# Linear attention with a routed expert layer: three numerator accumulators, the selection moved to ScalarE, GpSimd's first order bound, and gathered rows transposed as fp32r

## The chip, the cores and the metric

The kernel runs on one core of one Trainium2 chip. A core has TensorE (PE: matrix products; PEld is its load of the stationary operand), VectorE (DVE), ScalarE (ACT), GpSimd (POOL) and SyncE (SP, which issues most transfers). The metric is the time of one execution on the device in microseconds (us); lower is better. A second number, the span, is the time that the trace of a profiled execution covers.

## The reference

Linear attention over 8 batches, 8 heads, 576 positions and head size 64, and behind it a layer of 8 experts in which each of the 4608 rows goes to the one expert with the largest logit.

```python
def phi(x):
    proj = einsum('bhsd,df->bhsf', x, w_phi)                    # 128 features
    proj = proj - max(abs(proj), axis=-1, keepdims=True)
    return concatenate([exp(proj), exp(-proj)], axis=-1)
kv  = einsum('bhsf,bhsd->bhfd', phi(k), v)
z   = sum(phi(k), axis=2)
num = einsum('bhsf,bhfd->bhsd', phi(q), kv)
den = einsum('bhsf,bhf->bhs', phi(q), z)[..., None] + 1e-06
x   = rows of num / den                                          # 4608 x 512
logits = x @ w_gate                                              # 8 experts
expert = argmax(logits); gate = softmax(logits)[expert]
out[row] = gate[row] * (relu(x[row] @ w1[expert]) @ w2[expert])  # 512 -> 1024 -> 512
```

## The kernel before

The attention is cut into 16 units: 4 groups `g` of two batches, and in each group 4 pairs of heads `pr`. Most products run as three products in the type fp32r: a value is split into a rounded part (`xh`, `vh`, `kh`, `wh`) and a residual (`xl`, `vl`, `kl`, `wl`), and high x high, high x low and low x high are summed in PSUM. The rounding is a copy on ScalarE, the residual a subtraction on VectorE or GpSimd.

In a unit, `split` (L243, L244) cuts loaded pieces of q and k into `xh` and `xl`; `project` (L255 to L257) makes the feature projections `ps_proj`; VectorE takes the maximum `mx` (L261) and subtracts it (`t`, L262); ScalarE makes the exponentials `e` (L274, L275), and `k_parts` makes `kh` (L282, ScalarE) and `kl` (L284, on GpSimd for pieces 4 and 6, and for piece 0 from unit 1 on). For q, `t` is transposed on TensorE (`pt`, L293) and ScalarE writes the exponentials `qp`, or `qz` for the last, half chunk. `v_parts` makes `vh` (ScalarE, L311) and `vl` (GpSimd, L312). The products of k and v (`pk`, L336) gather kv for one batch; ScalarE copies them (`kvT`, L353), and a product with `fold` (`pf`, L362: identity columns and a block of `w_gate`) gives `kf`, which VectorE copies. The numerators, 9 chunks of 128 rows by 2 heads, are `pn` (L386; L395 for the tail chunk of both batches). Each has 73 columns: 64 of the result, one denominator, 8 logits. They stand in PSUM accumulators of six slots of 73 columns; one unit fills four (chunks 0 to 2, 3 to 5, 6 and 7, and the tail), and two accumulators exist at a time. `normalize` and `normalize_tail` divide them on VectorE (`rec`, `xrow`, `lgc`; L423 to L458), and `xrow` goes to a table in DRAM.

The routing of a group (`route`) sums the logits of the 4 pairs, takes the expert, counts rows per expert, gives each row its rank, and writes selection matrices: for each of the 9 chunks, `sel_p` on VectorE and `sel_h` on GpSimd (L788), each one comparison of an index row with the chunk's rank `rkr`, times a value. Of the last group's chunks some are written on ScalarE instead (L780 to L782). For the first three groups the routing's steps are `deferred`: they are laid between the products of the units that follow the group (about 150, 250 and 350 us). Only the last group's routing, near 420 to 445 us, stands between two stages.

Then come 17 pair units of two gathered blocks each (256 rows), and single blocks. `x_parts` transposes a gathered block `xg` in four pieces on TensorE into `px` (L1078) and splits it on ScalarE and VectorE (L1080, L1081); the first layer is `pm` (L1098 to L1100), the second `po` (L1118 to L1120), and the weights are split as they arrive (`wh` L1053, `wl` L1054).

A scheduler of the framework sets the order of each engine's instructions from the order of the code, priorities and dependences; `ordered` chains the products of TensorE, and `behind(m, other)` sets an instruction behind another on one engine without a wait. `merge` and `zipped` lay the features of a unit between the products of the one before. `constants` and the first unit's features begin the kernel.

```python
if u % NPR == 0 and u > 0:
    run(deferred)
    deferred = route(st["g"] - 1, units[u - 1]["lgc"], 0, NC)
```

Of the kernel before, what the change touches and what calls it, by code (L numbers as in the profile page):

```python
# [37 lines left out]
NSLOT = 7  # L38
NEARLY = (NG - 1) * NC
# [10 lines left out]
def tile_linear_attention_moe(  # L50
# [20 lines left out]
    make_identity(nc, ident)  # L71
    gidx = keep.tile([P, NB], I32, name="gidx")
# [58 lines left out]
    def constants():  # L131

        G.memset(fold, 0.0)
        for h in range(H):
            G.tensor_copy(fold[:, h, 0 : D + 1], ident[0 : D + 1, 0 : D + 1])
        nc.scalar.dma_start(fold[0:D, :, D + 1 : W], w_gate.rearrange("(h d) e -> d h e", d=D))

    def constants2():

        G.memset(ltri, 1.0)  # L140
        G.affine_select(ltri, ltri, [[1, P]], ALU.is_gt, 0.0, base=0, channel_multiplier=-1)

        G.iota(iota_i, [[1, P]], base=0, channel_multiplier=0)
        G.tensor_copy(iota_p, iota_i)
        G.tensor_copy(iota_pb, iota_i)
        G.tensor_scalar_add(iota_em, iota_e, -float(E))
        G.iota(part_i, [[0, 1]], base=1, channel_multiplier=1)
        G.tensor_copy(part1, part_i)


        G.iota(hb_i[:, :, 0:4], [[18, NG], [2, 4]], base=0, channel_multiplier=0)
        G.iota(hb_i[:, :, 4:8], [[18, NG], [2, 4]], base=9, channel_multiplier=0)
        G.iota(hb_i[0:64, :, 8:9], [[18, NG], [0, 1]], base=8, channel_multiplier=0)
        G.iota(hb_i[64:P, :, 8:9], [[18, NG], [0, 1]], base=16, channel_multiplier=0)
        G.tensor_copy(hbase, hb_i.rearrange("p g c -> p (g c)"))
        G.tensor_scalar_mul(hbase, hbase, 64.0)
        G.tensor_scalar_mul(neg1, part1, -1.0)
        G.tensor_scalar_mul(neg_h, hbase, -1.0)

# [77 lines left out]
    def split(st, x, part, eh, el):  # L237
# [6 lines left out]
        el.tensor_tensor(xl[:, 0:n], xr[:, 0:n], xh[:, 0:n], op=ALU.subtract)  # L244
# [33 lines left out]
    def k_parts(st, c0, n):  # L278
# [5 lines left out]
        eng.tensor_tensor(kl, e[:, 0:m], kh, op=ALU.subtract)  # L284
# [22 lines left out]
    def v_parts(st, u):  # L307
# [4 lines left out]
        G.tensor_tensor(vl, vt, vh[:, :, 0:D], op=ALU.subtract)  # L312
# [65 lines left out]
    def num_steps(st, chunks):  # L378


        def step(c, hh, s):
            if c in (0, 3, 6, 8) and hh == 0 and s == 0:
                st["pn"] = ps_nm.tile([P, 6, W], F32, name="pn")
            qp, s0 = st["qp", c]
            if c < 8:
                m = T.matmul(  # L386
                    st["pn"][:, 2 * (c % 3) + hh, :],
# [5 lines left out]
            else:  # L393

                m = T.matmul(  # L395
                    st["pn"][:, 2 * hh : 2 * hh + 2, :],
# [5 lines left out]
            if c in (2, 5, 7, 8) and hh == 1 and s == 1:  # L402
                if c < 8:
                    normalize(st, c - c % 3, c % 3 + 1, st["pr"])
                else:
                    normalize_tail(st, st["pr"])
# [11 lines left out]
    def normalize(st, c0, n, pr):  # L418
        pn = st["pn"][:, 0 : 2 * n]
        if c0 == 0:  # L420
            st["x"] = hold.tile([P, NC, P], F32, name="xrow", bufs=2)
        rec = sm.tile([P, 6], F32, name="rec", bufs=2)[:, 0 : 2 * n]
        V.tensor_scalar_add(rec, pn[:, :, D], 1e-6)  # L423
        V.reciprocal(rec, rec)
        rb = rec.rearrange("p (c h) -> p c h", h=2).unsqueeze(3)
        V.tensor_tensor(
            st["x"][:, c0 : c0 + n, :].rearrange("p c (h d) -> p c h d", h=2),
            pn[:, :, 0:D].rearrange("p (c h) d -> p c h d", h=2),
            rb.to_broadcast([P, n, 2, D]),
            op=ALU.mult,  # L430
        )
        V.tensor_tensor(
            st["lgc"][:, c0 : c0 + n, 2 * pr : 2 * pr + 2, :],
            pn[:, :, D + 1 : W].rearrange("p (c h) e -> p c h e", h=2),
            rb.to_broadcast([P, n, 2, E]),
            op=ALU.mult,
        )

    def normalize_tail(st, pr):

        pn = st["pn"][:, 0:4].rearrange("p (h b) w -> p h b w", b=2)
        rec = sm.tile([P, 6], F32, name="rec", bufs=2)[:, 0:4].rearrange("p (h b) -> p h b", b=2)
        V.tensor_scalar_add(rec, pn[:, :, :, D], 1e-6)
        V.reciprocal(rec, rec)
        for b in range(2):
            rows = slice(D * b, D * b + D)
            V.tensor_tensor(
                st["x"][rows, 8, :].rearrange("p (h d) -> p h d", h=2),
                pn[rows, :, b, 0:D],
                rec[rows, :, b].unsqueeze(2).to_broadcast([D, 2, D]),  # L450
                op=ALU.mult,
            )
            V.tensor_tensor(
                st["lgc"][rows, 8, 2 * pr : 2 * pr + 2, :],
                pn[rows, :, b, D + 1 : W],
                rec[rows, :, b].unsqueeze(2).to_broadcast([D, 2, E]),
                op=ALU.mult,
            )  # L458
# [188 lines left out]
    def route(g, lgc, c0, n, final=None):  # L647
# [13 lines left out]
        def logits():  # L661
            V.tensor_reduce(
                tile_of("lg", [P, NC, E]),
                lgc[:, c0 : c0 + n].rearrange("p c h e -> p c e h"),
                axis=AX.X,
# [118 lines left out]
        def select(c):  # L784
            if final is not None and c0 + c in ON_ACT:
                return select_a(c)
            for eng, dst, by in ((V, sel_p, part1), (G, sel_h, hbase[:, j0 + c : j0 + c + 1])):
# [129 lines left out]
    for g in range(NG):  # L917
        lgc = sm.tile([P, NC, H, E], F32, name="lgc")
# [150 lines left out]
    def x_parts(u, i):  # L1069
# [7 lines left out]
        for k in range(KD):  # L1077
            T.transpose(px[:, k, :], xg[:, k * P : (k + 1) * P], ident)  # L1078
# [277 lines left out]
```

## Time and profile before

| | |
|---|---|
| time before, median of 3 runs | 924.06 us (922.11 to 924.46) |
| the profiled execution's own time | 923.96 us |
| its span, instructions | 922.3 us, 18298 |
| mean granted clock of TensorE | 0.983 of full speed |
| TensorE busy | 889.5 us, 96% |
| VectorE, ScalarE, GpSimd busy | 596.7, 590.5, 485.0 us |
| attention units, about | 0 to 410 us |
| last numerators and last routing, about | 410 to 455 us |
| pair units, single blocks, about | 455 to 815 us, 815 to 905 us |

The busy time of an engine is the sum of its instructions' durations, overlaps counted once. The granted clock tells at which share of its full speed TensorE was let run: in a stretch with a low number, each product takes longer. In a row of a timeline, the first two numbers are start and duration in us; a bracket behind a row tells how long the engine was idle before it and what ended the idle time. In rows of groups, `x41` is the number of instructions, then come total us and mean ns.

### The profile page before, as it was taken

What the parts mean: (1) busy time and instruction counts of PE and PEld (TensorE: products, weight loads), DVE (VectorE), ACT (ScalarE), POOL (GpSimd) and SP (SyncE); (2) the same over time, 40 slices, a digit from 0 to 9 for tenths busy, and PEclk for the clock granted to TensorE, in tenths of its full rate; (3) what the DMA queues carried; (4) which work ended last, traced back from release to release, by engine and by line L of the source; (5) the groups of instructions that cost most, each with busy time, mean ns of one, the idle gap of its engine ahead of it and who ended that gap; (6) DMA issues with size and microseconds to landing.
All of it is one profiled execution on the core that took longest, in us unless ns stands there. A gap on an engine that the chain in (4) does not pass through costs nothing. (4 is left out here: it accounts for less than half of the span.)

```text
span 922.3 us, 18298 instructions
## 1 busy us (share of the span) xinstructions
PE 889.5 (96%) x6703; PEld 831.0 (90%) x6703; DVE 596.7 (65%) x1134; ACT 590.5 (64%) x900; POOL 485.0 (53%) x332
## 2 busy tenths in 40 slices
PE   7799999999999999999999999999999999999995
PEld 6799999999999999999799999999999999987883
DVE  7477788777987788759774444444444444457850
ACT  7577787777868776755565555555555555568951
POOL 7556668866676669734443333333333333337641
PEclk9799999999999999999999999999999999999998
DMA  5233433233334333243143143431434634764100
GB/s 154 80 96 107 107 106 103 68 100 102 93 93 108 106 107 93 76 129 108 59 154 122 45 152 115 155 112 44 153 114 158 215 113 149 229 206 129 46 24 15
DMA packets 64620, 102.44 MB, mean 111 GB/s; under 512 B 10702, under 2 KB 28622, under 8 KB 64528
## 3 DMA queue, kind: packets, MB, share of 16 engines
q1 hardware_dynamic: 57136, 80.31, 28.5%
q0 software_dynamic: 6720, 20.80, 7.3%
q8 instruction: 53, 0.87, 0.4%
q14 instruction: 39, 0.32, 0.1%
q10 hardware_dynamic: 672, 0.15, 0.1%
HBM read 136.81 MB, written 20.26 MB: 170 GB/s over the span
## 5 line engine op out<-in xcount | busy, mean ns | idle before, releaser
L1054 DVE TENSOR_TENSOR wl<-raw,wh 128x1024 fp32r<-128x1024 f32 x138 | 184.6, 1350 | 136.2 <-ACT wh L1053 136.1
L1053 ACT CAST wh<-raw 128x1024 fp32r<-128x1024 f32 x184 | 191.4, 1050 | 93.7 <-PE po L1120 66.2
L1054 POOL TENSOR_TENSOR wl<-raw,wh 128x1024 fp32r<-128x1024 f32 x46 | 113.3, 2469 | 175.0 <-ACT wh L1053 167.6
L386 PE MATMUL pn<-kf,qp 128*128 128x73 f32 x1024 | 156.8, 252 | 0.0
L1099 PE MATMUL pm<-xl,wh 128*128 128x256 f32 x544 | 154.1, 283 | 0.0
L1100 PE MATMUL pm<-xh,wl 128*128 128x256 f32 x544 | 154.1, 283 | 0.0
L1098 PE MATMUL pm<-xh,wh 128*128 128x256 f32 x544 | 153.4, 283 | 0.0
L386 PEld LDWEIGHTS pn<-kf,qp 128*128 128x128 f32 x1024 | 151.3, 190 | 0.1
L284 POOL TENSOR_TENSOR kl<-e,kh 128x1024 fp32r<-128x1024 f32 x47 | 112.4, 2392 | 50.7 <-ACT kh L282 47.9
L261 DVE TENSOR_REDUCE mx<-ps_proj 128x4 f32<-128x512 f32 (+1 forms) x160 | 101.2, 633 | 43.8 <-PE ps_proj L257 43.1
L244 POOL TENSOR_TENSOR xl<-xr,xh 128x512 fp32r<-128x512 f32 (+2 forms) x63 | 88.0, 1403 | 69.6 <-ACT xh L243 69.5
L1118 PE MATMUL po<-wh,hh 128*128 128x512 f32 x272 | 108.9, 401 | 0.0
L1119 PE MATMUL po<-wl,hh 128*128 128x512 f32 x272 | 106.8, 392 | 1.1 <-DVE wl L1054 1.1
L1099 PEld LDWEIGHTS pm<-xl,wh 128*128 128x128 f32 x544 | 104.1, 191 | 2.8 <-DVE xl L1081 0.4
L1098 PEld LDWEIGHTS pm<-xh,wh 128*128 128x128 f32 x544 | 104.0, 191 | 2.5
L1120 PE MATMUL po<-wh,hl 128*128 128x512 f32 x272 | 106.1, 390 | 0.0
L336 PE MATMUL pk<-kl,vh 128*65 128x256 f32 x320 | 99.8, 312 | 4.9 <-POOL kl L284 4.1
L1100 PEld LDWEIGHTS pm<-xh,wl 128*128 128x128 f32 x544 | 104.1, 191 | 0.2 <-issue 0.2
L262 DVE TENSOR_TENSOR t<-ps_proj,mx 128x512 f32<-128x512 f32 (+1 forms) x160 | 99.9, 632 | 3.2
L336 PE MATMUL pk<-kh,vh 128*65 128x256 f32 x320 | 100.6, 314 | 0.0
L336 PE MATMUL pk<-kh,vl 128*64 128x256 f32 x320 | 100.4, 314 | 0.0
L255 PE MATMUL ps_proj<-w_hi,xh 128*128 128x256 f32 x288 | 90.2, 313 | 4.2 <-DVE t L262 2.4
(232 smaller groups left out, 2010.9 us busy)
## 6 DMA issues: line engine op xcount, KB each, us to landing
raw<-w SPq DMA_DIRECT2D x184, 512.0 KB
vt<-vv SPq DMA_DIRECT2D x15, 640.0 KB
x_dram<-xrow SPq DMA_DIRECT2D x30, 256.0 KB
xr<-kT SPq DMA_DIRECT2D x15, 320.0 KB
xr<-qT SPq DMA_DIRECT2D x15, 320.0 KB
xr<-kT SPq DMA_DIRECT2D x17, 256.0 KB
xr<-qT SPq DMA_DIRECT2D x17, 256.0 KB
x_dram<-xrow SPq DMA_DIRECT2D x32, 32.0 KB
```

Of the source, the lines that this page charges most:

```text
L261: V.tensor_reduce(mx[:, 0 : 2 * n], psv, axis=AX.X, op=ALU.max, apply_absolute_value=True)
L284: eng.tensor_tensor(kl, e[:, 0:m], kh, op=ALU.subtract)
L336: return T.matmul(st["pk", bb][0:n, hh, :], (vl if j == 1 else vh)[:, 2 * (c + (bb if c == 8 else 0)) + hh, 0:n], (kl if j == 2 else kh)[: ...
L386: m = T.matmul(st["pn"][:, 2 * (c % 3) + hh, :], qp[:, s, s0 + hh, :], st["kf"][:, c // 4, hh, s, :], start=(s == 0), stop=(s == 1),)
L1053: A.copy(th, raw[k])
L1054: m = (G if k in (POOL_LO if u else POOL_LO0) else V).tensor_tensor(tl, raw[k], th, op=ALU.subtract)
L1098: T.matmul(pm[:, i], th, xh[:, k, :], start=(k == 0), stop=False)
L1099: T.matmul(pm[:, i], th, xl[:, k, :], start=False, stop=False)
L1100: T.matmul(pm[:, i], tl, xh[:, k, :], start=False, stop=(k == KD - 1))
L1118: T.matmul(po, hh[:, i, r], th[:, c], start=(i == j == 0), stop=False)
L1119: T.matmul(po, hh[:, i, r], tl[:, c], start=False, stop=False)
L1120: T.matmul(po, hl[:, i, r], th[:, c], start=False, stop=(i == 1 and j == 3))
```

## The change

It has four parts.

Three accumulators: a unit's numerators fill three accumulators of seven slots in turn instead of four of six. The index `i = 2 * c + hh` counts chunk and head; the third accumulator holds the last two ordinary slots and the tail's four. `normalize` takes an accumulator's first index and does what `normalize_tail` did too, and `lgc` is laid out by pair, so that the logits' sum runs over two axes.

Selection: in the routing of the first three groups, `sel_p` is written on ScalarE by two activations, `y` = |index - rank| and relu(part - part * y), which is `part` where the index is the rank, and zero elsewhere. `sel_h` stays on GpSimd. The last group's routing keeps its code.

GpSimd's first order: the clearing of `fold` is set behind the residual of k's third part of unit 0, the residual of unit 1's first part of k behind the `kl` of piece 4 of unit 0, and the `vl` of unit 1 behind the `kl` of piece 0.

Transposes: those of the gathered rows read and write their data as fp32r, with an fp32r copy of the identity that is made on GpSimd among the constants.

```diff
+SLOTS = 7
...
+    ident_r = keep.tile([P, P], F32R, name="ident_r")
...
-        G.memset(fold, 0.0)
+        behind(G.memset(fold, 0.0), units[0]["xl", "k", 2])
...
+        G.tensor_copy(ident_r, ident)
...
-        el.tensor_tensor(xl[:, 0:n], xr[:, 0:n], xh[:, 0:n], op=ALU.subtract)
+        m = el.tensor_tensor(xl[:, 0:n], xr[:, 0:n], xh[:, 0:n], op=ALU.subtract)
+        st["xl", x, part] = m
+        if (st["u"], x, part) == (1, "k", 0):
+            behind(m, units[0]["kl", 4])
...
-        eng.tensor_tensor(kl, e[:, 0:m], kh, op=ALU.subtract)
+        st["kl", c0] = eng.tensor_tensor(kl, e[:, 0:m], kh, op=ALU.subtract)
...
-        G.tensor_tensor(vl, vt, vh[:, :, 0:D], op=ALU.subtract)
+        m = G.tensor_tensor(vl, vt, vh[:, :, 0:D], op=ALU.subtract)
+        if u == 1:
+            behind(m, st["kl", 0])
...
-            if c in (0, 3, 6, 8) and hh == 0 and s == 0:
-                st["pn"] = ps_nm.tile([P, 6, W], F32, name="pn")
+            i = 2 * c + hh
+            if i % SLOTS == 0 and c < 8 and s == 0:
+                st["pn"] = ps_nm.tile([P, SLOTS, W], F32, name="pn")
...
-                    st["pn"][:, 2 * (c % 3) + hh, :],
+                    st["pn"][:, i % SLOTS, :],
...
-                    st["pn"][:, 2 * hh : 2 * hh + 2, :],
+                    st["pn"][:, 2 + 2 * hh : 4 + 2 * hh, :],
...
-            if c in (2, 5, 7, 8) and hh == 1 and s == 1:
-                if c < 8:
-                    normalize(st, c - c % 3, c % 3 + 1, st["pr"])
-                else:
-                    normalize_tail(st, st["pr"])
+            if s == 1 and (i % SLOTS == SLOTS - 1 or i == 17):
+                normalize(st, i - i % SLOTS, st["pr"])
+                if c == 8:
...
+    def normalize(st, i0, pr):
...
+        last = i0 == 2 * SLOTS
+        m = 6 if last else SLOTS
+        n = 2 if last else SLOTS
+        rec = sm.tile([P, SLOTS], F32, name="rec", bufs=2)
+        V.tensor_scalar_add(rec[:, 0:m], pn[:, 0:m, D], 1e-6)
+        V.reciprocal(rec[:, 0:m], rec[:, 0:m])
...
+        def divide(rows, dst, slots):
+            k = dst.stop - dst.start
+            r = rec[rows, slots].unsqueeze(2)
+            for t, c0, c1 in ((x, 0, D), (lg, D + 1, W)):
+                V.tensor_tensor(
+                    t[rows, dst], pn[rows, slots, c0:c1], r.to_broadcast([rows.stop - rows.start, k, c1 - c0]), op=ALU.mult
+                )
+
+        divide(slice(0, P), slice(i0, i0 + n), slice(0, n))
+        if last:
+            for b in range(2):
+                divide(slice(D * b, D * b + D), slice(16, 18), slice(2 + b, 6, 2))
...
-            for eng, dst, by in ((V, sel_p, part1), (G, sel_h, hbase[:, j0 + c : j0 + c + 1])):
+            by = hbase[:, j0 + c : j0 + c + 1]
+            if final is None:
+                y = sg.tile([P, P], F32, name="y", bufs=2)
+                A.activation(y, iota_p, AF.Abs, bias=r["rkr"][:, c : c + 1], scale=-1.0)
+                A.activation(sel_p[:, j0 + c, :], y, AF.Relu, bias=part1, scale=neg1)
+            for eng, dst, by in ((G, sel_h, by),) if final is None else ((V, sel_p, part1), (G, sel_h, by)):
...
-        lgc = sm.tile([P, NC, H, E], F32, name="lgc")
+        lgc = sm.tile([P, NPR, 2 * NC, E], F32, name="lgc")
...
-            T.transpose(px[:, k, :], xg[:, k * P : (k + 1) * P], ident)
+            T.transpose(px[:, k, :].bitcast(F32R), xg[:, k * P : (k + 1) * P].bitcast(F32R), ident_r)
```

The order of the instructions moves with it. GpSimd (POOL) at the start, behind the constants; `vl_171` is unit 1's, the `xl` of 640 columns behind it is unit 1's too, and the two `kl` behind are unit 0's. Before:

```order
L156 TENSOR_SCALAR hbase<-hbase 128x36 [waits Pool_49]
L158 TENSOR_SCALAR neg_h<-hbase 128x36 [waits Pool_49]
L244 TENSOR_TENSOR xl<-xr,xh 128x512 [waits DMAHW2_49,PE_49,Activation_49]
L312 TENSOR_TENSOR vl_171<-vt,vh_169 128x1280 [waits DMAHW4_49,Activation_49]
L244 TENSOR_TENSOR xl<-xr,xh 128x640 [waits DMAHW3_49,PE_49,Activation_49]
L284 TENSOR_TENSOR kl<-e,kh 128x1024 [waits Activation_49] x2
L244 TENSOR_TENSOR xl<-xr,xh 128x640 [waits DMAHW5_49,PE_49,Activation_49]
L244 TENSOR_TENSOR xl<-xr,xh 128x512 [waits DVE_49,DMAHW6_49,PE_49,Activation_49]
```

The same place now, where `ident_r` has joined the constants some rows ahead and `vl_172` is unit 1's:

```order
L158 TENSOR_SCALAR hbase<-hbase 128x36 [waits Pool_49]
L160 TENSOR_SCALAR neg_h<-hbase 128x36 [waits Pool_49]
L247 TENSOR_TENSOR xl<-xr,xh 128x512 [waits DMAHW1_49,PE_49,Activation_49]
L290 TENSOR_TENSOR kl<-e,kh 128x1024 [waits Activation_49]
L247 TENSOR_TENSOR xl<-xr,xh 128x640 [waits DMAHW2_49,PE_49,Activation_49]
L247 TENSOR_TENSOR xl<-xr,xh 128x640 [waits DMAHW5_49,PE_49,Activation_49]
L290 TENSOR_TENSOR kl<-e,kh 128x1024 [waits Activation_49]
L247 TENSOR_TENSOR xl<-xr,xh 128x512 [waits DVE_49,DMAHW6_49,PE_49,Activation_49]
L290 TENSOR_TENSOR kl<-e,kh 128x1024 [waits Activation_49]
L247 TENSOR_TENSOR xl<-xr,xh 128x512 [waits PE_49,DMAHW7_49,Activation_49,Pool_49]
L318 TENSOR_TENSOR vl_172<-vt,vh_170 128x1280 [waits DMAHW4_49,Activation_49]
```

The first `kl` of unit 0 has moved ahead of unit 1's `vl` and `xl`, and `vl` stands behind three `kl`.

GpSimd at the first group change, the routing's steps among the residuals of the units around; `onehot`, `base`, `sel_h` and `gt` are the routing's. Before:

```order
L709 CAST onehot<-oh_b 128x72 [waits DVE_49]
L738 TENSOR_TENSOR base<-base,gsum 128x8 [waits DVE_49]
L284 TENSOR_TENSOR kl<-e,kh 128x1024 [waits Activation_49]
L244 TENSOR_TENSOR xl<-xr,xh 128x640 [waits PE_49,DMAHW1_49,Activation_49,Pool_49]
L312 TENSOR_TENSOR vl_168<-vt,vh_166 128x1280 [waits DMAHW4_49,Activation_49]
L244 TENSOR_TENSOR xl<-xr,xh 128x512 [waits PE_49,DMAHW7_49,Activation_49,Pool_49]
L788 TENSOR_SCALAR sel_h<-iota_pb,rkr,hbase 128x128 [waits DVE_49]
L788 TENSOR_SCALAR sel_h<-iota_pb,rkr,hbase 128x128 x4
L284 TENSOR_TENSOR kl<-e,kh 128x1024 [waits Activation_49]
L788 TENSOR_SCALAR sel_h<-iota_pb,rkr,hbase 128x128 x4
L809 COPY gt<-se 128x36 [waits DVE_49]
L244 TENSOR_TENSOR xl<-xr,xh 128x512 [waits PE_49,DMAHW0_49,Activation_49,Pool_49]
```

The same place now:

```order
L701 CAST onehot<-oh_b 128x72 [waits DVE_49]
L730 TENSOR_TENSOR base<-base,gsum 128x8 [waits DVE_49]
L247 TENSOR_TENSOR xl<-xr,xh 128x640 [waits PE_49,DMAHW0_49,Activation_49,Pool_49]
L247 TENSOR_TENSOR xl<-xr,xh 128x640 [waits PE_49,DMAHW1_49,Activation_49,Pool_49]
L290 TENSOR_TENSOR kl<-e,kh 128x1024 [waits Activation_49]
L318 TENSOR_TENSOR vl_169<-vt,vh_167 128x1280 [waits DMAHW2_49,Activation_49]
L785 TENSOR_SCALAR sel_h<-iota_pb,rkr,hbase 128x128 [waits DVE_49]
L785 TENSOR_SCALAR sel_h<-iota_pb,rkr,hbase 128x128 x8
L290 TENSOR_TENSOR kl<-e,kh 128x1024 [waits Activation_49]
L806 COPY gt<-se 128x36 [waits DVE_49]
L290 TENSOR_TENSOR kl<-e,kh 128x1024 [waits Activation_49,Pool_49]
L247 TENSOR_TENSOR xl<-xr,xh 128x512 [waits PE_49,DMAHW7_49,Activation_49,Pool_49]
```

All nine `sel_h` stand ahead of the next `kl`, where five did, and an `xl` of 512 columns has moved behind them.

VectorE (DVE) at the same group change, from the ranks (`blk`, `rkr`) on, with the normalization (`rec`, `xrow`, `lgc`) of the numerators `pn`. Before:

```order
L763 CAST blk<-prki 128x9 [waits DVE_49]
L764 CAST rkr<-prki 128x9
L423 TENSOR_SCALAR rec<-pn 128x6 [waits PE_49]
L788 TENSOR_SCALAR sel_p<-iota_pb,rkr,part_145 128x128 [waits DVE_49]
L788 TENSOR_SCALAR sel_p<-iota_pb,rkr,part_145 128x128
L424 RECIPROCAL rec<-rec 128x6 [waits DVE_49]
L788 TENSOR_SCALAR sel_p<-iota_pb,rkr,part_145 128x128
L426 TENSOR_TENSOR xrow<-pn,rec 128x384 [waits DVE_49]
L432 TENSOR_TENSOR lgc<-pn,rec 128x3x16
L788 TENSOR_SCALAR sel_p<-iota_pb,rkr,part_145 128x128 x3
L423 TENSOR_SCALAR rec<-pn 128x4 [waits PE_49]
```

The same place now:

```order
L755 CAST blk<-prki 128x9 [waits DVE_49]
L756 CAST rkr<-prki 128x9
L268 TENSOR_TENSOR t<-ps_proj,mx 128x512 [waits DVE_49]
L434 TENSOR_SCALAR rec<-pn 128x7 [waits PE_49]
L435 RECIPROCAL rec<-rec 128x7 [waits DVE_49]
L443 TENSOR_TENSOR xrow<-pn,rec 128x448 [waits DVE_49]
L443 TENSOR_TENSOR lgc<-pn,rec 128x56
L267 TENSOR_REDUCE mx<-ps_proj 128x2 [waits PE_49]
L268 TENSOR_TENSOR t<-ps_proj,mx 128x256 [waits DVE_49,Activation_49]
L434 TENSOR_SCALAR rec<-pn 128x6 [waits PE_49]
L435 RECIPROCAL rec<-rec 128x6 [waits DVE_49]
L267 TENSOR_REDUCE mx<-ps_proj 128x2 [waits PE_49]
```

The selections are gone from VectorE, and the normalization of seven slots follows the ranks with one projection's `t` between.

On ScalarE the nine pairs of `y` and `sel_p` stand in ones and twos among the `e`, `qp`, `kh` and `kvT` of that unit, ahead of some of each.

More of the change, by code (lines that the diff above doesn't have):

```diff
@@ L416, in num_steps @@
         ]
-    def normalize(st, c0, n, pr):
-        pn = st["pn"][:, 0 : 2 * n]
-        if c0 == 0:
+    def normalize(st, i0, pr):
+        pn = st["pn"]
+        if i0 == 0:
             st["x"] = hold.tile([P, NC, P], F32, name="xrow", bufs=2)
[L422 to L458, printed above, removed]
+        last = i0 == 2 * SLOTS
@@ new lines, in normalize @@
+        m = 6 if last else SLOTS
[3 more added lines that the diff above has]
+        V.reciprocal(rec[:, 0:m], rec[:, 0:m])
+        x = st["x"].rearrange("p c (h d) -> p (c h) d", h=2)
+        lg = st["lgc"][:, pr]
+        def divide(rows, dst, slots):
[5 more added lines that the diff above has]
+                )
@@ L663, in logits @@
                 tile_of("lg", [P, NC, E]),
-                lgc[:, c0 : c0 + n].rearrange("p c h e -> p c e h"),
-                axis=AX.X,
+                lgc[:, :, 2 * c0 : 2 * c0 + 2 * n].rearrange("p r (c h) e -> p c e r h", h=2),
+                axis=AX.XY,
                 op=ALU.add,
```

## The prediction

> **What bounds the kernel now.** The busy times and the slices of the page come first.
>
> ```profile
> PE 889.5 (96%) x6703; PEld 831.0 (90%) x6703; DVE 596.7 (65%) x1134; ACT 590.5 (64%) x900; POOL 485.0 (53%) x332
> ...
> PE   7799999999999999999999999999999999999995
> ...
> PEclk9799999999999999999999999999999999999998
> ```
>
> TensorE is busy for 889.5 of 922.3 us, so only three things can make the kernel faster: idle time of TensorE, time at a lowered clock, or cheaper work on TensorE. A second list, of what TensorE waited for, names the idle time.
>
> ```profile
> PE pn L395 <- DVE lgc L432: 5.8, 3, 1.9
> PE pk L336 <- POOL kl L284: 4.1, 1, 4.1
> ...
> PE ps_proj L255 <- ACT xh L243: 1.8, 1, 1.8
> ```
>
> The columns are total us, times, longest. Three waits of 1.9 us for a normalization on VectorE, and one of 4.1 us for a residual on GpSimd, lead it. A table of windows shows what they cost (window and length; then busy us of PE, weight loads, DVE, ACT, POOL with instruction counts; then the granted clock, DMA share, GB/s).
>
> ```profile
> 22.00:27.00 5.00, 0.92 (x8) 0.67 (x7) 1.81 (x3) 1.44 (x3) 4.55 (x3) 1.00 0.61 198
> 27.00:31.00 4.00, 4.00 (x23) 3.81 (x21) 1.66 (x3) 2.95 (x5) 1.66 (x1) 0.57 0.02 8
> 31.00:35.00 4.00, 1.55 (x9) 1.14 (x8) 0.57 (x2) 3.92 (x9) 2.27 (x2) 0.87 0.00 0
> 35.00:40.00 5.00, 5.00 (x27) 5.00 (x27) 3.11 (x6) 1.13 (x5) 1.27 (x1) 0.50 0.44 131
> 96.00:120.00 24.00, 23.84 (x223) 23.48 (x223) 18.36 (x43) 18.68 (x33) 15.41 (x9) 1.00 0.39 103
> 152.00:160.00 8.00, 6.06 (x42) 5.86 (x41) 7.00 (x20) 2.80 (x8) 8.00 (x8) 0.80 0.77 226
> 350.00:358.00 8.00, 6.09 (x44) 5.90 (x43) 7.09 (x20) 2.21 (x5) 8.00 (x8) 0.80 0.70 209
> 140.00:165.00 25.00, 23.06 (x206) 22.77 (x205) 21.92 (x61) 16.25 (x31) 21.51 (x18) 0.93 0.34 98
> 600.00:620.00 20.00, 20.00 (x136) 18.50 (x135) 8.27 (x9) 10.33 (x14) 6.87 (x4) 1.00 0.32 107
> ```
>
> A normal attention unit (96 to 120 us) and the pair stage (600 to 620) leave TensorE full at full clock: there only cheaper TensorE work counts. After each wait the clock is cut for a few us: 0.57 and 0.50 in the start, 0.80 over the 8 us of a group change. So a wait costs more than its length. At the group change TensorE issued 42 instructions in 8 us where a normal unit issues 223/24 x 8 = 74, so 32 / 9.3 per us = 3.5 us are lost, three times: 10.5 us.
>
> **Part 1, the selection on ScalarE.** The timeline of VectorE, GpSimd and TensorE at the first group change:
>
> ```profile
> 151.53 3.52 DVE L788 TENSOR_SCALAR sel_p<-iota_pb,rkr,part 128x128 bf16<-128x128 bf16 x2
> 154.97 0.18 DVE L424 RECIPROCAL rec<-rec 128x6 f32<-128x6 f32 x1
> 155.86 0.19 DVE L432 TENSOR_TENSOR lgc<-pn,rec 128x48 f32<-128x48 f32 x1
> ...
> 151.08 2.69 POOL L312 TENSOR_TENSOR vl<-vt,vh 128x1280 fp32r<-128x1280 f32 x1
> 153.74 1.25 POOL L244 TENSOR_TENSOR xl<-xr,xh 128x512 fp32r<-128x512 f32 x1
> 158.99 2.38 POOL L284 TENSOR_TENSOR kl<-e,kh 128x1024 fp32r<-128x1024 f32 x1
> ...
> 156.20 0.49 PE L395 MATMUL pn<-kf,qz 128*128 128x146 f32 x2 [1.94 <-DVE lgc L432]
> 164.50 0.32 PE L336 MATMUL pk<-kl,vh 128*65 128x256 f32 x1
> ```
>
> Two `sel_p` take 3.52 us, and end (155.05) when GpSimd's `vl` and `xl` end (154.99). Behind them wait the reciprocal and `lgc`, and TensorE's tail product, which needs the accumulator back. The same selections, by source line over the group change, and ScalarE's two instructions for one selection, from the final route:
>
> ```profile
> L788 DVE TENSOR_SCALAR sel_p<-iota_pb,rkr,part x9: 300/370/2299, 151.5 to 158.1; 128x128 bf16<-128x128 bf16 x9
> L788 POOL TENSOR_SCALAR sel_h<-iota_pb,rkr,hbase x9: 781/791/1293, 155.0 to 164.2; 128x128 bf16<-128x128 bf16 x9
> ...
> L781 ACT ACTIVATE sel_p<-y,part,neg 128x128 bf16<-128x128 f32 x5 | 2.4, 483 | 0.0
> L780 ACT ACTIVATE y<-iota_p,rkr 128x128 f32<-128x128 f32 x5 | 1.8, 392 | 0.1
> ```
>
> One selection lasts 300 ns beside an idle GpSimd and up to 2299 beside a busy one (minimum, median, maximum). The Trainium skill, "SBUF — State Buffer", section "Who interferes with whom", says that VectorE and GpSimd share a port pair, that a VectorE scalar operation in its two-port mode and a GpSimd instruction exclude each other for a whole instruction, and that ScalarE never waits; the trace agrees in 2299 against 300 ns, and by that rule the selections on ScalarE would wait for nobody.
>
> The change takes all 27 off VectorE, so the place that stalls is gone: up to 10.5 us. What it puts in place: 9 x (0.39 + 0.48) = 7.9 us of ScalarE per group at most. ScalarE has 25.00 - 16.25 = 8.7 us idle in the window of the group change, 3.5 of them in the stall that goes, so 5.2: it fits only by running 2.7 us into the next unit, which has 24.00 - 18.68 = 5.3. Queued behind selections are `kvT`, `e` and `kh`; each pair that is in front costs such a step up to 1 us or so, and TensorE waits for `kvT`.
>
> GpSimd is the closer one: 21.51 busy of 25.00, and with the stall gone 21.5 in 21.5. The nine `sel_h` stand now all ahead of the `kl` that ran at 158.99, before only five. That is 4 x 0.79 = 3.2 us, less the `xl` of 1.25 now behind it: 1.9 us later. It ended at 161.37 and was used at 164.50, 3.1 us of slack, all of it (3.5) lent by the stall. So TensorE may wait up to 1.9 + 0.4 = 2.3 us, or not at all if the queue starts earlier. I take 1.7 given back per group, `kvT` and a little clock included. Gain 3 x (3.5 - 1.7) = 5.4 us; ends: 10.5, and a loss of 3 x 0.8 = 2.4 where a 2.3 us wait costs what 1.94 did and more (4.3 by the same ratio of 3.5/1.94).
>
> **Part 2, three accumulators.** VectorE loses two small instructions per unit, 32 in all, on an engine with 18.36 of 24 busy: nothing on the path. The tail product joins accumulator three, which was given back when the first seven slots had been normalized, long before; so it no longer waits for the normalization just ahead. That secures part 1's gain but adds none in units that had no wait. The last group's route begins after a larger accumulator: up to two products' worth later, plus 0.5 us (ends 0 and 1).
>
> **Part 3, GpSimd's first order.** Timeline of the start:
>
> ```profile
> 18.79 1.30 POOL L244 TENSOR_TENSOR xl<-xr,xh 128x512 fp32r<-128x512 f32 x1
> 20.05 2.72 POOL L312 TENSOR_TENSOR vl<-vt,vh 128x1280 fp32r<-128x1280 f32 x1
> 22.72 1.54 POOL L244 TENSOR_TENSOR xl<-xr,xh 128x640 fp32r<-128x640 f32 x1
> 24.21 2.34 POOL L284 TENSOR_TENSOR kl<-e,kh 128x1024 fp32r<-128x1024 f32 x1
> ...
> 20.39 1.04 ACT L282 CAST kh<-e 128x1024 fp32r<-128x1024 f32 x1
> ...
> 26.61 0.34 PE L336 MATMUL pk<-kl,vh 128*65 128x256 f32 x1 [4.08 <-POOL kl L284]
> 35.44 0.54 PE L362 MATMUL pf<-fold,kvT 65*128 65x73 f32 x2
> ```
>
> `vl` and `xl` of the next unit stand ahead of a `kl` whose `kh` was there at 21.43. Now `kl` comes right behind the first `xl`. With the copy of the identity on the same queue (an estimate of 0.3 us, a quarter of this `xl` of four times its columns, and 1.3 at most) `xl` ends near 20.9, `kl` runs from 21.5 to 23.9, and TensorE goes on at 24.0: 2.6 us earlier. Behind it lies the cut clock: 4 x 0.43 = 1.7 us in 27 to 31 and 5 x 0.50 = 2.5 in 35 to 40, and 4 - 1.55 = 2.45 us idle in 31 to 35. What is late next is `xl` of unit 1 and its `xh` (the 1.8 us wait in the list), which the change doesn't hasten. I count 2.6, a half of the clock loss (2.1) and 0.8 of the second idle stretch: 5.5 us. Ends: 2 (the copy and the memset shift the queue by as much as 0.6 more and every clock loss stays) and 2.6 + 1.7 + 2.5 + 1.2 = 8. The moved memset and `vl` are covered by GpSimd's idle time after 26.5; `fold` is first read at 35.44, in the last row. ScalarE's cast of unit 1's `vh` moves back with `vl` and hastens nothing that is waited for.
>
> **Part 4, transposes as fp32r.** Pair stage, and the groups' rows:
>
> ```profile
> 601.92 0.28 PE L1100 MATMUL pm<-xh,wl 128*128 128x256 f32 x1
> 602.04 0.60 PE L1078 MATMUL px<-ident,xg 128*128 128x128 f32 x4
> 602.40 0.47 PE L1118 MATMUL po<-wh,hh 128*128 128x512 f32 x1
> 602.71 0.40 PE L1119 MATMUL po<-wl,hh 128*128 128x512 f32 x1
> 602.95 0.40 PE L1120 MATMUL po<-wh,hl 128*128 128x512 f32 x1
> ...
> L1078 PE MATMUL px<-ident,xg 128*128 128x128 f32 x164 | 25.0, 273 | 0.8 <-DMA xg<-x_dram,gidx 0.8
> ```
>
> `L1118` leads to the next after 0.31 us instead of 0.24, so four transposes take 0.36 + 0.07 = 0.43 us, 108 ns each, 17.7 us over 164. An fp32r product of 256 columns takes 0.12 us and one of 512 0.24, so 128 columns would take 55 to 60 ns at that rate: at most 164 x 51 ns = 8.4 us saved. The other end is zero: one instruction each before and after, and the weight loads stay. I take the middle, 26 ns each, 4.2 us, since neither an fp32r product of 128 columns nor an fp32 one of 256 stands in the trace to decide it. All of it lies on the path (20.00 busy of 20).
>
> The Trainium skill, "TensorE: Matmul & The Clock Gate", section "LDWEIGHTS (loading the stationary operand)", gives a load as its columns over 1.2 in ns, whatever the type's speed in the array. By it a transpose of 128 columns is bound near 107 ns by its load, part 4 brings nothing, and the sum below would be 913.6; the trace has 108 ns for a transpose, but also 0.12 us for the fp32r product of twice the columns with a load of the same size, so that it cannot decide. The zero is a rival below.
>
> **The sum.** The profiled execution took 923.96 us, 0.1 below the median of 924.06. 923.96 - 5.4 + 0.5 - 5.5 - 4.2 = 909.4.
>
> **Rivals.** First, transposes no cheaper: 913.6. For it: the load of equal size. Against: the load of the fp32r product hides in 0.12 us. Second, transposes at the full fp32r rate: 909.4 - 4.2 = 905.2. Third, the group change brings nothing net: TensorE waits about 1.9 us for `kl` or `kvT` instead of `lgc`, so 909.4 + 5.4 = 914.8. For it: GpSimd full at 21.5 of 21.5. Fourth, on the other side: GpSimd becomes the bound of the route units. Then `kl`, and behind it the two `xl` that the selections push back, are each late, two waits per group with a cut clock each, 2 x 3.5 = 7 us for the 3.5 saved: +10.5, and with part 3 at its low end of 2 and transposes unchanged 933. It decides against the change only where TensorE waits over 1.94 + 5.5/3 x 0.55 = 2.9 us per group, where 0.55 is 1.94/3.5, the wait behind a lost us, and 5.5 is part 3; that is more than the 2.3 us found above. Fifth, nothing acts: the start's wait passes to `xl` and `xh` of unit 1 and the group's to `kl`, transposes unchanged: 923 to 924.
>
> **How the numbers follow.** Chances: forecast 0.42, first rival 0.2, second 0.14, third 0.12, fourth 0.06, fifth 0.06. A measurement here tells a change from none from about 0.3%, 2.8 us. The first four cases lie below 921: 0.88, less 0.02 for their edges; the fifth is no change, with those edges 0.07; the fourth slower, 0.07. The range: low end 899, all four terms near their better ends (8.5, 8 and 8.4 for parts 1, 3 and 4); high end 921, a third rival with a zero in part 4 and 3 us left of part 3. About 0.15 is left out.
>
> **What would show it.** Right: no wait of the tail product for `lgc` in the list; `sel_p` on ScalarE near 0.48 us; VectorE's group change without an instruction over 2 us; clock 0.9 or more there; first `pk` wait for `kl` under 2 us, ended by 24.5; `pf` before 33; after the transposes the next product within 0.3 us. Wrong: new waits of `pk` for `kl` or of `pf` for `kvT` of 2 us and more around 150, 250 and 350; a start wait that reappears under another name; transposes still 108 ns apart.

## The result, and the profile after

The changed kernel took 928.58 us (median of 7, 926.94 to 931.71) against 924.06 for the kernel before: the ratio is 1.0059, interval 1.0042 to 1.0077. It is a little slower, where 15 us less had been forecast. The profiled execution took 928.25 us, its span is 926.5.

The page's first lines, as they stood for the kernel before:

```profile
PE 888.1 (96%) x6703; PEld 826.7 (89%) x6703; DVE 588.6 (64%) x1075; ACT 607.5 (66%) x954; POOL 480.3 (52%) x333
...
PE   8999998999989998998999999999999999999995
...
PEclk7999999999989999999999999999999999999998
```

The hole of the start (second slice, 7 tenths busy before) is gone; new shallow dips of 8 tenths stand at the three group changes (slices 7, 12 and 16) and at the last routing (slice 19). The list of what TensorE waited for gives them names:

```profile
PE ps_proj L263 <- POOL xl L247: 7.7, 6, 2.1
PE pn L395 <- DVE kf L381: 2.7, 6, 0.5
...
PE pk L344 <- POOL kl L290: 2.4, 4, 0.8
PE pt L299 <- ACT y L782: 2.1, 3, 0.7
```

The 5.8 us for `lgc` and the 4.1 us for the first `kl` have left the list. In their place TensorE waits 7.7 us for `xl` from GpSimd, 2.7 for `kf`, and three times 0.7 for a transpose `pt`. By windows (columns as before):

```profile
25.00:30.00 5.00, 4.00 (x34) 3.62 (x32) 4.06 (x8) 4.41 (x11) 3.51 (x2) 1.00 0.38 118
35.00:40.00 5.00, 5.00 (x49) 5.00 (x48) 3.80 (x6) 4.40 (x8) 4.41 (x3) 1.00 0.28 88
96.00:120.00 24.00, 23.49 (x220) 23.23 (x220) 18.67 (x40) 18.47 (x32) 15.04 (x9) 1.00 0.38 103
152.00:160.00 8.00, 6.91 (x62) 6.44 (x60) 6.96 (x11) 5.54 (x13) 3.63 (x4) 1.00 0.07 2
160.00:168.00 8.00, 5.43 (x33) 4.93 (x32) 3.42 (x5) 4.33 (x8) 4.44 (x3) 0.82 0.28 76
```

The start runs at full clock from 20 us on. The group change lost its old hole and has two new ones, the second with a cut clock, and the ordinary unit lost 0.35 us of busy time (23.49 against 23.84).

Where it went is told best by the moments at which each unit's first `pk` is issued (every 60th `pk` in the timeline; for pairs and blocks the first `pm`), after minus before:

| at | difference, us | so that stretch gave |
|---|---|---|
| unit 1 | -9.2 | start: -9.2 |
| unit 5 | -8.2 | four ordinary units: +1.0 |
| unit 6 | -5.3 | first group change: +2.9 |
| unit 9 | -3.8 | three ordinary units: +1.4 |
| unit 10 | -0.6 | second group change: +3.2 |
| unit 13 | +1.4 | three ordinary units: +2.0 |
| unit 14 | +3.4 | third group change: +2.0 |
| fourth pair | +5.3 | last units, last routing: +1.9 |
| first single blocks | +3.7 | 14 pairs: -1.5 |
| end | +4.3 | rest: +0.6 |

The start gave nine, the three group changes took eight, and the other units with the last routing six.

At the first group change the timeline of GpSimd, TensorE, VectorE and ScalarE reads:

```profile
145.66 7.03 POOL L785 TENSOR_SCALAR sel_h<-iota_pb,rkr,hbase 128x128 bf16<-128x128 bf16 x9
152.64 2.39 POOL L290 TENSOR_TENSOR kl<-e,kh 128x1024 fp32r<-128x1024 f32 x1
...
159.61 2.37 POOL L290 TENSOR_TENSOR kl<-e,kh 128x1024 fp32r<-128x1024 f32 x1 [2.36 <-ACT kh L288]
161.95 2.49 POOL L247 TENSOR_TENSOR xl<-xr,xh 128x512 fp32r<-128x512 f32 x2
...
150.08 0.41 PE L299 MATMUL pt<-ident,t 128*128 128x128 f32 x2 [0.71 <-ACT y L782]
...
163.26 0.39 PE L263 MATMUL ps_proj<-w_hi,xl 128*128 128x256 f32 x1 [2.07 <-POOL xl L247]
164.50 0.39 PE L263 MATMUL ps_proj<-w_hi,xl 128*128 128x256 f32 x1 [0.49 <-POOL xl L247]
...
149.50 0.42 DVE L268 TENSOR_TENSOR t<-ps_proj,mx 128x256 f32<-128x256 f32 x1
...
153.09 2.50 DVE L290 TENSOR_TENSOR kl<-e,kh 128x512 fp32r<-128x512 f32 x1
...
155.06 0.63 ACT L280 ACTIVATE e<-t 128x512 f32<-128x512 f32 x1 [2.46 <-POOL kl L290]
159.37 1.14 ACT L246 CAST xh<-xr 128x512 fp32r<-128x512 f32 x2
```

Nine `sel_h` hold GpSimd for 7.03 us; `kl` begins only at 152.64; until it ends ScalarE can't write the next `e` and idles 2.46 us; its `kh` and `xh` are late; and GpSimd, which has been told to do another `kl` ahead of the two `xl`, waits for that `kh` and does the `xl` last. The first wait, 0.71 us of `pt`, is put down to a `y`, but the `t` that `pt` reads was ready at 149.92, only 0.1 us before that `y` ended; `t` had stood behind the division of the numerators on VectorE. TensorE's waits here add up to 0.71 + 0.79 + 0.30 + 2.07 + 0.49 = 4.36 us, and 3.41 us at half clock follow (1.7 us): 6.1 us at this group change, against 1.94 + 1.7 = 3.6 before.

### The profile page after: what moved, and what is told of

Same layout as the page of the kernel before. It is cut to its first block, busy times and chain, and to the rows that moved or that the text cites. A ratio compares the mean times of both kernels' runs of the same rounds, so it can differ in the third digit from the quotient of the medians.

```text
span 926.5 us, 18307 instructions
## 1 busy us (share of the span) xinstructions
PE 888.1 (96%) x6703; PEld 826.7 (89%) x6703; DVE 588.6 (64%) x1075; ACT 607.5 (66%) x954; POOL 480.3 (52%) x333
## 5 line engine op out<-in xcount | busy, mean ns | idle before, releaser
L395 PE MATMUL pn<-kf,qp 128*128 128x73 f32 x1024 | 160.8, 255 | 2.7 <-DVE kf L381 2.7
L395 PEld LDWEIGHTS pn<-kf,qp 128*128 128x128 f32 x1024 | 153.8, 193 | 4.6 <-DVE kf L381 4.5
```

The lines of the kernel that those rows point to most:

```text
L395: m = T.matmul(st["pn"][:, i % SLOTS, :], qp[:, s, s0 + hh, :], st["kf"][:, c // 4, hh, s, :], start=(s == 0), stop=(s == 1),)
```

## The experiments

All ran beside the kernel before on the same chip. Ratios are against it, with their intervals.

**The parts one by one.** First each of the four parts alone in the kernel before. The order only:

```diff
+        behind(G.memset(fold, 0.0), units[0]["xl", "k", 2])
+        if (st["u"], x, part) == (1, "k", 0):
+            behind(m, units[0]["kl", 4])
+        if u == 1:
+            behind(m, st["kl", 0])
```

> Only GpSimd's first order is changed, everything else as before. In the changed kernel the products of the second unit began 9.2 us earlier. If the order of GpSimd's first residuals alone does that (theory), the start's 4.08 us wait of pk for kl and the cut clock behind it go and stay gone to the end: 924 - 9 = 915 us, 913 to 918. Rival: the nine us came partly from the first accumulator's other size or from a clock that differs from run to run, then 918 to 924.

914.73 us, ratio 0.9898 (0.9861 to 0.9936). The start's gain is real, comes from GpSimd's order alone, and stays to the end. In the profile 8.4 us of it stand at the second unit's first `pk`; some 2 more came at the first two group changes, where the wait for `lgc` is as long as before and the clock wasn't cut (the last section shows why).

The selection only (`select` as in the change):

> Only the selection of the first three groups goes to ScalarE. Theory, the queue of GpSimd: the loss at a group change needs the nine sel_h in one block ahead of kl, and that block comes with the three accumulators; here five stand ahead of kl and four behind, as before, so the 1.94 us waits go and only short waits stay (pt for y 0.7, xl under 1): each group change gains 1.5 to 3, 924 - 4.5 to 9 = 915 to 920 us. Rival, ScalarE: nine pairs of activations delay kh and xh by themselves, then xl is 2 us late here too, with its cut clock, 6.1 against 3.65 us lost per group: 924 + 7 = 931 us.

922.41 us, ratio 0.9986 (0.9969 to 1.0004): nothing that can be measured, and neither theory's number. The wait for `lgc` is gone, but its place is taken; list of waits, then the group change (GpSimd, ScalarE, TensorE):

```profile
PE ps_proj L257 <- POOL xl L244: 5.5, 4, 1.6
...
166.21 2.38 POOL L284 TENSOR_TENSOR kl<-e,kh 128x1024 fp32r<-128x1024 f32 x1 [0.79 <-ACT kh L282]
168.54 1.27 POOL L244 TENSOR_TENSOR xl<-xr,xh 128x512 fp32r<-128x512 f32 x1
...
166.02 0.62 ACT L243 CAST xh<-xr 128x512 fp32r<-128x512 f32 x1
...
169.86 0.38 PE L257 MATMUL ps_proj<-w_hi,xl 128*128 128x256 f32 x1 [1.63 <-POOL xl L244]
```

`xh` is there at 166.64, but `kl` stands ahead of `xl`: the scheduler set the two the other way round than before.

The three accumulators only:

> Only the three accumulators. Theory: the ordinary units lose 0.3 to 0.5 us each, since the first numerator waits for kf (VectorE), some 5 us over the units, and the nine sel_h now in one block make kl late at group changes; against that the tail product waits no longer for lgc. Together 924 + 5 + (-6 to +4) = 923 to 933 us. Rival, the accumulators only help: no wait of the tail product at the group changes, about 3.5 us each: 914 us.

936.55 us, ratio 1.0140 (1.0103 to 1.0177): 12 us, more than the worst that was expected. List of waits, and GpSimd and TensorE at the first group change:

```profile
PE pk L337 <- POOL kl L285: 11.9, 4, 3.8
...
PE pn L388 <- DVE kf L374: 1.9, 5, 0.5
...
153.15 7.68 POOL L773 TENSOR_SCALAR sel_h<-iota_pb,rkr,hbase 128x128 bf16<-128x128 bf16 x9
160.80 1.26 POOL L245 TENSOR_TENSOR xl<-xr,xh 128x512 fp32r<-128x512 f32 x1
162.02 2.34 POOL L285 TENSOR_TENSOR kl<-e,kh 128x1024 fp32r<-128x1024 f32 x1
...
164.42 0.47 PE L337 MATMUL pk<-kl,vh 128*65 128x256 f32 x1 [3.78 <-POOL kl L285]
```

The block of nine `sel_h` comes with the accumulators, not with the selection: with another layout of the numerators the scheduler draws the four last `sel_h` ahead of `kl` of piece 6.

The transposes only:

> Only the transposes of the gathered rows as fp32r, with the copied identity. The pair stage of the changed kernel gave 14 ns per transpose, 164 x 14 = 2.3 us: 921.7 us (theory). By the mean duration of a transpose, which fell by 26 ns, 919.8 us (rival). If the copy of the identity on GpSimd delays the start, 924 or more.

920.15 us, ratio 0.9957 (0.9938 to 0.9976), 4 us. Its pair stage gains 0.22 us for every 16 transposes, 14 ns each or 2.3 us in all; the rest (1.5 to 2 us) came in the attention's end and at a group change whose clock wasn't cut, so the theory's 14 ns holds and the time agrees rather with the rival.

**The two orders on GpSimd.** The selection alone, with `xl` of q's second part put back ahead of `kl` of piece 0:

```diff
-                items += [ks[8], qs[8], kps[8], ks[0], qs[0], kps[0]]
-        items.append(do(v_parts, st, u))
+                items += [ks[8], qs[8], kps[8], ks[0], qs[0]]
+        items += [kps[0], do(v_parts, st, u)]
...
+        if c0 == 0 and st["u"] > 0:
+            behind(st["kl", 0], st["xl", "q", 1])
```

> The selection alone on ScalarE, as before, but GpSimd is made to take xl of q's second part ahead of kl of piece 0 in the unit behind a group change, as it did in the kernel before. Theory: with the selection alone the gain was given back by one wait of 1.6 us for this xl per group, only because kl stood ahead of it; with the order back the wait goes or stays under 0.6 us, the clock is not cut, and some 2.5 to 3.3 us per group come out: 922.4 - 7.5 to 10 = 913 to 915 us. Rival: xh is late on ScalarE itself, behind selections and exponentials, so another order on GpSimd saves a few tenths: 921 to 922 us.

917.08 us, ratio 0.9922 (0.9894 to 0.9949), between the theory and the rival and nearer to the theory. The order was bound in every unit behind the first, not only behind a group change. The waits for `xl` at the group changes are gone and nothing over 0.5 us took their place. ScalarE had room for the selections; the order behind them took the gain.

The accumulators alone, with four `sel_h` behind `kl` of piece 6 (`G` is GpSimd, `c` the chunk):

```diff
+                if final is None and eng is G:
+                    kl6 = units[NPR * g + NPR + 1].get(("kl", 6))
+                    if kl6 is not None and c > 4:
+                        behind(m, kl6)
```

> The three accumulators alone, as before, but four of the nine sel_h are set behind kl of piece 6, as in the kernel before. Theory: the block of nine sel_h makes kl 3 to 3.8 us late in each group; with five ahead it comes 3.2 us earlier, the wait shrinks under 1 us and the cut clock goes: 3 x 3 to 5 = 9 to 15 us less than the 936.5 with accumulators alone, 922 to 927 us. What is left over 924 is the ordinary units' wait for kf. Rival: the selections on VectorE are what holds up the rest, and kl is late with five as with nine: 933 to 937 us.

929.83 us, ratio 1.0058 (1.0031 to 1.0085), 6.7 less than with the block. The wait for `kl` falls from over 3 to under 0.3 us, and the attention ends 11 us earlier than with the accumulators alone. At each group change 0.9 us of wait for a `t` are left, and a new wait takes part of the gain back near 473 us:

```profile
PE pm L1088 <- DVE xl L1070: 3.5, 1, 3.5
```

The change without the accumulators:

> The whole change without the three accumulators: four of six slots again. If the accumulators are what turned the sum (theory), this is 924.2 - 9.5 (first order) - 4.1 (fp32r) - 1.8 (selection) = 909 us, 907 to 911. Rival: selection, first order and transposes disturb each other too, and the time lies between 912 and 924 us.

912.98 us, ratio 0.9880 (0.9834 to 0.9927): the accumulators turned the sum, since with them the same kernel took 928.58. Against the additive number 4 us are missing, so the time lies in the rival's range, at its fast end; the three waits of 1.6 us for `xl` stand here as with the selection alone.

The whole change with both orders put back:

> The whole change, with GpSimd's order at the group change put back in two places: four of nine sel_h behind kl of piece 6, and xl of q's second part ahead of kl of piece 0. Theory: the 2.07 and 0.5 us waits for xl and the 0.8 us for kl go with their cut clock, 3 x 4 to 5.5 us less than the 928.6 of the change: 912 to 917 us; left over against the version without accumulators is the wait for kf in the ordinary units, 4 to 5 us. Rival, ScalarE holds the features up by itself: 924 to 928 us.

925.89 us, ratio 1.0009 (0.9987 to 1.0031). The theory's 912 to 917 was wrong; the time is the rival's, but its reason isn't what the list shows. The `xl` waits are down from 2.07 to 0.6 us, but `kf` now costs more than the 4 to 5 us that were allowed, and the 3.6 us wait for a block's `xl` near 473 us is here too. List of waits:

```profile
PE pn L397 <- DVE kf L383: 5.5, 7, 1.6
PE pm L1102 <- DVE xl L1084: 3.6, 1, 3.6
```

**What was left.** The version without accumulators, with `xl` first:

> The change without the three accumulators (913.0), and with xl of q's second part ahead of kl of piece 0. Theory: the three waits of 1.6 us for xl go as they did with the selection alone, and nothing takes their place; the clock wasn't cut there in the profile without accumulators, so 3 x 1.6 = 4.9 us: 908 us, 906 to 910, the fastest of all. Rival: ScalarE's late xh shows up elsewhere: 911 to 913.

906.68 us, ratio 0.9823 (0.9784 to 0.9863), the fastest of all, 1.8% under the kernel before. Its two longest entries in the list of waits are one of the first 20 us that all these kernels have, and six short ones of a transpose:

```profile
PE ps_proj L260 <- DVE t L267: 2.8, 2, 1.6
PE pt L300 <- DVE t L267: 2.8, 6, 0.7
```

The change without the selection:

> The whole change but the selection, which stays on VectorE. If the parts add up (order -9.5, transposes -4.1, accumulators +12.3), 922.9 us, and the selection would have cost 5.7 in the company of the accumulators. Theory: nine sel_h stand ahead of kl of piece 6 here as with the accumulators alone, a wait of 3 us and over per group, so 921 to 925. Rival: with the start 9 us earlier the waits fall otherwise and selections on VectorE are the better place: under 918.

931.68 us, ratio 1.0083 (1.0044 to 1.0121), slower than expected. It lies 3 us above the whole change, with intervals that overlap; three waits of 3 us and over for `kl` stand here as in the accumulators alone. Yet up to the last unit it is the faster of the two: its first `pk` there comes at 397.7 us, against 401.0 in the whole change. It loses its lead behind that, in a wait for a block's `xl` near 479 us, which the whole change has only with 0.9 us:

```profile
PE pm L1091 <- DVE xl L1073: 3.5, 1, 3.5
```

So within the attention of these two profiles the selection on ScalarE made the change dearer, by some 3 us, and the whole time hides it.

The reordered change, with `kf` ahead of `kl` of piece 8 on VectorE:

```diff
+                if bb == 0 and st["u"] + 1 < len(units):
+                    behind(units[st["u"] + 1]["kl", 8], m_kf)
```

> The whole change with GpSimd's order put back in two places (925.9), and kf of a unit's first batch ahead of kl of piece 8 on VectorE. Theory: what was left of the accumulators' cost in the units is the first numerator's wait for kf, 0.3 to 0.5 us in ordinary units and 1.55 with a cut clock (3.3 together) in two or three units behind a group change; with kf first they go: 925.9 - (8 x 0.4 + 2 x 3.3) = 916 us, 914 to 919. The wait of 3.6 us for xl of a block near 472 us (with its cut, 5 to 7 us) is not touched, and stays. Rival: kl of piece 8 becomes late instead and the wait has only another name: 923 to 926.

914.32 us, ratio 0.9901 (0.9869 to 0.9934). Every wait for `kf` over 0.2 us went, and 11.6 us with them. The attention is now as fast as in the fastest version: the last unit's first `pk` comes at 379.9 against 380.6 us. The theory had 914 to 919. The block's wait stays, as said; list of waits, and VectorE and GpSimd in front of it:

```profile
PE pm L1104 <- DVE xl L1086: 3.5, 1, 3.5
...
455.92 4.52 DVE L1059 TENSOR_TENSOR wl<-raw,wh 128x1024 fp32r<-128x1024 f32 x2
...
456.43 2.93 POOL L1059 TENSOR_TENSOR wl<-raw,wh 128x1024 fp32r<-128x1024 f32 x1 [3.85 <-ACT wh L1058]
```

And that wait too:

```diff
+        m = V.tensor_tensor(xl, px, xh, op=ALU.subtract)
+        if (u, i) == (2, 1):
+            for w in wls[-2:]:      # the last residuals of weights on VectorE
+                behind(w, m)
```

> The version of 914.3 us (the whole change, GpSimd's order put back in two places, kf first), and two residuals of weights (wl) on VectorE set behind xl of the third pair's second block. Theory: the 3.55 us wait of pm for this xl and the cut clock behind it (1.7 us) come from two wl that take 4.5 instead of 2.4 us beside a wl on GpSimd; with xl ahead they go: 914.3 - 5 = 909 us, 907 to 911, and what then parts it from the version without accumulators (906.7) is the 1.7 us wait of pm for hl near 415 us with its cut clock. Rival: the two wl become late for po and the wait moves there: 913 to 915.

909.87 us, ratio 0.9851 (0.9810 to 0.9891). The wait is gone; one of 1.2 us for a gathered block stands near 472 us now. From the 928.6 of the change, four orders of instructions lead to 910, with all its parts kept. What parts it from 906.7 comes behind the last unit: there its loss against the fastest version grows by 2.5 us up to the second pair, in a wait of 1.65 us of `pm` for `hl` and three short ones in the last routing.

## Why the prediction was wrong

The parts, as the prediction priced them and as they came out:

| part | predicted, us | alone, us | in the change |
|---|---|---|---|
| selection | -5.4 | -1.8 (not measurable) | group changes: +8.1 with the accumulators |
| accumulators | +0.5 | +12.3 | about +16 (913.0 to 928.6), of it ordinary units and last routing about +6 |
| first order | -5.5 | -9.5 | start: -9.2 |
| transposes | -4.2 | -4.1 | pairs: -1.5, about -2 in all |

Alone the four parts add up to -3.1 us, together they gave +4.5: they aren't independent, while the prediction added them up.

**Part 2, accumulators: the step that failed.** "Nothing on the path" counted VectorE's instructions, two fewer per unit, and asked only who waits for the accumulator. It didn't ask what the new layout does to the order of all else, and what then runs beside what. Two things came of it. The first is the block of nine `sel_h` ahead of `kl` (3 to 3.8 us of wait per group alone, with the cut clock behind it). The second is `kf`. VectorE took it behind `kl` of piece 8 before as well, and this `kl` was short; now a `kl` of GpSimd runs beside it, it is longer by 0.56 us, and the first numerator, which stands closer behind the fold than before, waits 0.51 us. One ordinary unit, first the kernel before, then the changed one:

```profile
109.58 0.69 DVE L284 TENSOR_TENSOR kl<-e,kh 128x512 fp32r<-128x512 f32 x1
...
99.48 2.38 POOL L290 TENSOR_TENSOR kl<-e,kh 128x1024 fp32r<-128x1024 f32 x1
...
101.16 1.25 DVE L290 TENSOR_TENSOR kl<-e,kh 128x512 fp32r<-128x512 f32 x1
102.33 0.45 DVE L381 COPY kf<-pf 128x292 f32<-128x292 f32 x1
...
102.83 0.44 PE L395 MATMUL pn<-kf,qp 128*128 128x73 f32 x2 [0.51 <-DVE kf L381]
```

Over all units this `kl` takes 1291 ns in the mean, against 734 before, and 694 in the run that sets `kf` first. Which of the two, the longer `kl` or the closer numerator, weighs more was not parted. That these orders cost the time is shown by binding each by itself: four `sel_h` behind `kl` gave about 7 us back in the accumulators alone, and `kf` first gave 11.6 in the reordered change, whose waits for `kf` were twice those of the change (5.5 against 2.7 us). The tail product's own wait for `lgc` is indeed gone, as was said.

**Part 1, selection.** Right: no wait for `lgc`; 396 and 492 ns per activation (392 and 483 predicted); ScalarE holds the work; no `sel_p` stalls on VectorE any more. Wrong: two of its signs, since a `kl` of VectorE's lasts 2.50 us at the group change and the clock of the second hole is 0.82; and what was given back. The 1.7 us were worked out for `kl` of piece 6 alone; that the `xl` behind it would be the later one was priced only in the rival on the other side. It said that GpSimd becomes the bound and `kl` and the two `xl` are each late, and gave it 0.06 with 7 us per group. The late ones are the right ones, and the trace shows 6.1 us; but GpSimd isn't the bound, with 3.63 and 4.44 of 8 us busy in the two holes: it waits for `kh` in a chain that goes through ScalarE. The prediction's own limit, 2.9 us of wait per group, was passed with 4.36. Since the order of GpSimd was in the text (nine `sel_h`, and `xl` behind), the chain from `kl` through `e`, ScalarE and `kh` to `xl` could have been followed a step further. One reading of the rows was wrong too: the selections of 300 ns did not stand beside an idle GpSimd. All nine ran while GpSimd was busy, the short ones beside `sel_h`, the two long ones beside `vl` and `xl`; why `sel_h` doesn't hold them up, no run shows. Two small slips change nothing: 2.3 us at the ratio 3.5/1.94 make 4.15 and not 4.3, and in Part 3 the terms put the end of `xl` at 20.4 and not 20.9.

**Part 3, first order.** Right in sign and mechanism, sized too small: 9.5 in the time and 8.4 to 9.2 at the second unit, against 5.5 and an end of 8. Only a half of the cut clock and 0.8 us of the second idle stretch were counted; in the change all of both went (2.6 + 4.2 + 2.45 = 9.25). First `pk` beyond the wait at 23.17 us (24.0 predicted), no cut clock between 20 and 40 us.

**Part 4, transposes.** The term's size came true in the time (4.1), by luck: about 2.3 us are the transposes' own, the rest came elsewhere, as said above. Pair stage of the changed kernel, and the group's row:

```profile
606.85 0.46 PE L1075 MATMUL px<-ident_r,xg 128*128 128x128 f32 x4
607.15 0.46 PE L1115 MATMUL po<-wh,hh 128*128 128x512 f32 x1
607.45 0.39 PE L1116 MATMUL po<-wl,hh 128*128 128x512 f32 x1
...
L1075 PE MATMUL px<-ident_r,xg 128*128 128x128 f32 x164 | 19.9, 241 | 0.2 <-DMA xg<-x_dram,gidx 0.2
```

Four take 0.30 + 0.07 = 0.37 us, 93 ns each against 108: 15 ns saved, not 26, and far from the 51 of the full rate; the first rival, no cheaper at 108 ns, didn't hold either. The mean duration did fall by 32 ns (241 against 273; the expectation above took 26), but the spacing is what counts on a full TensorE. What sets the 93 ns was not tried; the weight loads last 141 ns in both kernels.

The forecast of 909.4 is close to the 909.9 that the same parts give with the four orders bound. That is no proof of the prediction: what it left out, the orders, was 19 us.

## What to carry to other kernels

Where a scheduler orders the engines, an edit that saves instructions is priced by the order that comes out, not by the instructions: list what changed places on the engine with the longest instructions and what now runs beside it, and follow each late result through every buffer that it holds until a step of the bounding engine is reached. Then bind the two or three orders that matter by hand, since the next edit elsewhere will move them again. Before an edit is given up, try the old order with it: here the accumulators cost about 16 us in the change (928.6 against 913.0), and 3 with the orders bound (909.9 against 906.7).

## What the runs showed of the hardware

Whether a wait costs the clock depends on where it falls. From 20 to 880 us the stretches of half clock are whole multiples of 3.41 us, and in every run they begin on one grid of 3.41 us, whose offset differs from run to run. The kernel before and the one with the order alone have the same 1.94 us wait at the first group change. In the former all of it lies in one step of the grid, in the latter 0.7 and 1.2 us in two; windows around it, of the latter, at its first and third group change:

```profile
144.00:152.00 8.00, 6.06 (x55) 5.89 (x54) 8.00 (x23) 3.32 (x8) 8.00 (x8) 1.00 0.72 216
340.00:349.00 9.00, 7.08 (x51) 6.88 (x51) 7.45 (x23) 3.47 (x7) 9.00 (x8) 0.81 0.70 205
```

The first passes at full clock, with 55 instructions in 8 us where the kernel before had 42 at 0.80; the third, whole in one step, is cut. Over the fourteen profiles, from 20 to 880 us, each step of the grid with more than 1.8 us idle was followed by a cut one, none with less than 1.4 us unless it was cut itself, and between the two both occurred. So a wait near 2 us costs 2 or 3.7 us by its place, and some 2 us of a comparison of two kernels can come from that alone. The Trainium skill, "TensorE: Matmul & The Clock Gate", section "What's actually happening", says that the window is 3413 ns and free-running; the 3.41 us and the grid agree, but its condition of an idle window does not: a step a little more than half idle was enough here.

VectorE and GpSimd slow each other in two-input operations as well: two `wl` took 4.52 us beside a `wl` on GpSimd, which itself took 2.93 (rows of the experiment that sets `kf` first) where most take 2.4; in the changed kernel, where GpSimd's comes later, the same two read

```profile
473.01 2.34 DVE L1051 TENSOR_TENSOR wl<-raw,wh 128x1024 fp32r<-128x1024 f32 x2
```

and a `kl` of 512 columns took 2.50 us at the group change beside GpSimd's `kl` (rows of the result), against 0.69 without one. The Trainium skill, "SBUF — State Buffer", section "Who interferes with whom", says that an operation of two operands in SBUF contends with one of GpSimd that reads; both rows agree.
